# Pooled values of the first six pairs by matmul instead of by a second load, in an attention and mixture kernel on one Trainium2 core

## The chip, the cores and the metric

The kernel runs on one core of one Trainium2 chip. The metric is the device time of one execution in microseconds, the median of a few runs. Engines are named as in the profile: PE is TensorE (PEld its weight loads), DVE is VectorE, ACT is ScalarE, POOL is GpSimd, SP is SyncE, which issues the DMA transfers here.

## The reference, cut to what matters

Eight batches of eight heads with 576 positions of 64 numbers. Attention is the sum of a pooled one (means over 4 positions, repeated 4 times) and a banded one. Its output, with heads side by side, is the input x of a token-shifted feed-forward layer.

```python
q_d = q.reshape(B, H, Sd, 4, D).mean(axis=3)      # the same for k_d, v_d; Sd = 144
out_d = sm_attn(q_d, k_d, v_d)                    # softmax(q k / 8) v
out_up = np.repeat(out_d, 4, axis=2)
mask = np.abs(pos[:, None] - pos[None, :]) < 4
out_local = softmax(where(mask, q k / 8, -1e9)) @ v
x = (out_up + out_local)                          # B, S, H * D = 8, 576, 512
xk = mu_k * x + (1 - mu_k) * x_prev               # x_prev: x one position earlier
xr = mu_r * x + (1 - mu_r) * x_prev
k = np.maximum(xk @ w_k, 0.0)                     # 512 x 1024
v = k * k @ w_v                                   # 1024 x 512
out = sigmoid(xr @ w_r) * v                       # w_r: 512 x 512
```

The three weight matrices arrive as 64-bit floats; the rest is float32.

## The kernel before, in words

**Attention** runs over 32 pairs of heads (four pairs to a batch). `load_raw` fetches q and k of a pair in eight transfers, VectorE transposes them (`turn_q`, `turn_k`), GpSimd adds groups of four columns (`pool_q`, `pool_k`). TensorE computes the banded scores in 24 blocks (`score_pe`) and the pooled scores (`down_last`, `down_pe`) into one PSUM tile; the first four pairs add the mask by a matmul on the identity (L539). Softmax uses VectorE for maxima and sums, ScalarE for exponentials, GpSimd for normalising. `down_turn` transposes the pooled weights on TensorE, `down_copy` evicts them. The values are loaded twice: `load_windows` fetches the overlapping windows of the banded part (`vw`, 128 partitions: window i of 32 positions, 12 tiles of 64), and `load_v4` fetches four successive positions into one partition (`v4`), which GpSimd adds to pooled values (`pool_v`, L517 and L518, into `vd`). `av_pe` multiplies the pooled weights with `vd` (L671, L675) and the banded ones with `vw` (L681), in two row halves with a PSUM tile each. ScalarE evicts the pooled part (`av_up`), VectorE adds the other half's (`av_two`, L707), and `av_out` (L715) writes both into x.

**The feed-forward layer** runs over 18 chunks of 256 positions. Every weight and every x is split into a high and a low part, and three products are summed. A weight block (20 of them, in pairs of 32-bit words) is decoded by `weight_scale` (ScalarE, L377), then three VectorE instructions (L381, L385, L390), then `weight_high` (ScalarE), and the low part is made either by two matmuls on TensorE (`weight_diff`, L401 and L402, the first eight) or by GpSimd (`weight_low`). Mixing of chunk 0 runs on TensorE (`mix_pe`, L761: one call for each of xk and xr and each of four column groups), with ScalarE and VectorE splitting the result (L767, L771); later chunks mix on VectorE and ScalarE. `k_pe` (L800 for chunks 0 and 1, L804 and L806 after), `r_pe` (L850) and `v_pe` (L866) are the three products.

**What sets the order.** Each step is entered as a task with an engine, an assumed duration, what it reads and writes, and a rank. `Plan.order` simulates the five queues, and the rank, plus an entry of the table SHIFT, decides among tasks that could start. The instructions are then held in that order on each engine, DMA issues too. Where the plan sees TensorE idle in the first 100 us, `Plan.fill` puts filler matmuls on the identity (`keep_warm`, L408), as long as one of six PSUM banks is free.

Of the kernel before, what the change touches and what calls it, by code (L numbers as in the profile page):

```python
# [31 lines left out]
VDVE = 0  # L32
SPLIT = 8
# [17 lines left out]
    "r_pe.2": 136.8, "r_pe.3": 138.8, "s.av_out": -2.5, "s.av_two": -20.6, "s.av_up": -3.5, "s.diff": -5,  # L51
    "s.down_copy": 12.5, "s.down_top": -18.3, "s.down_turn": -11.7, "s.k_low": -27, "s.k_relu": -5,
    "s.k_sum": -22.9, "s.mix_add.xr": -105, "s.mix_high.xk": -11.4, "s.mix_low.xk": -44.3, "s.mix_part.xk": 5.4,
    "s.mix_part.xr": -6.5, "s.run_pe": -41.4, "s.score_top": -3.7, "s.score_turn": 16.2, "s.turn_k": 5.3,
# [1134 lines left out]
```

## Time and profile before

| | |
|---|---|
| median of 3 runs | 683.16 us (682.91 to 685.35) |
| the profiled execution | 687.01 us, span 685.2 us, mean granted clock 0.998 |
| busy | PE 660.1, DVE 509.5, ACT 480.8, POOL 295.4 us |
| moved by DMA | 62.19 MB, mean 91 GB/s |
| first k matmul of chunk 0 | 64.18 us |

"Busy" is the time in which an engine ran an instruction. A group row gives line, engine, operation, tiles (output<-input), shape and count, then total busy time and mean ns of one, then idle time before them and who ended it. A timeline row gives start, length, engine, line, tiles, count, and in brackets the idle time before. TensorE rows of plain float32 matmuls count two records for one instruction.

### The profile page before, as it was taken

To read this page: it belongs to the slowest core of one execution; us is meant where nothing else is said; L and a number is where in the kernel's file an instruction comes from. 1 tells how busy PE (TensorE), PEld (TensorE's weight loads), DVE (VectorE), ACT (ScalarE), POOL (GpSimd) and SP (SyncE) were. 2 spreads that over 40 slices of the span, in tenths; PEclk is the share of its full clock that TensorE was granted. 3 is DMA by queue.
4 is the path that set the end of the run, shared out by engine and by line. 5 is a ranking of instruction groups with operands and counts; after the bars stand their busy time and mean duration, and the time that the engine had idled before them with its cause. 6 is when DMAs were issued, how large, how long until landed. Compare 5 with 4: busy or idle time off the path is not lost.

```text
span 685.2 us, 18270 instructions
## 1 busy us (share of the span) xinstructions
PE 660.1 (96%) x7070; PEld 550.8 (80%) x7070; DVE 509.5 (74%) x1020; ACT 480.8 (70%) x1239; POOL 295.4 (43%) x375
## 2 busy tenths in 40 slices
PE   6888989999999999999999999999999999999997
PEld 4566778878788888888888888888888888888886
DVE  3879987889787997988657896599768984666222
ACT  4757877676877877886766767696859686755553
POOL 5545788754274355541515355452645331000000
PEclk9999999999999999999999999999999999999999
DMA  7998998754173435341415234532351100000000
GB/s 150 181 171 247 237 167 151 172 103 107 41 142 71 96 76 116 74 101 18 107 43 123 55 76 85 130 80 66 78 128 37 37 3 32 2 31 32 1 31 32
DMA packets 221593, 62.19 MB, mean 91 GB/s; under 512 B 204730, under 2 KB 214466, under 8 KB 221506
## 3 DMA queue, kind: packets, MB, share of 16 engines
q1 hardware_dynamic: 221506, 61.02, 42.0%
q8 instruction: 56, 0.92, 0.6%
q14 instruction: 31, 0.25, 0.1%
HBM read 51.55 MB, written 9.44 MB: 89 GB/s over the span
## 4 chain that ended last, share of the span: by engine, by line
PE 81%; DVE 9%; DMA 3%; ACT 3%; issue 2%; POOL 1%; SPq 1%; DVEq 0%; POOLq 0%; ACTq 0%
PE acc L866 27%; PE ps_g L804 16%; PE ps_r L850 14%; PE ps_g L806 8%; PE ps_v L681 3%; PE ps_a L544 3%; PE ps_v L671 2%; DMA kraw<-in_k_dram 2%; PE ps_a L611 1%; PE ps_g L800 1%; PE ps_a L604 1%; PE ps_a L549 1%; DMA wk<-in_moe_w_k_dram 1%; ACT L628 1%; PE ps_t L651 1%
## 5 line engine op out<-in xcount | busy, mean ns | idle before, releaser
L866 PE MATMUL acc<-wv,kh 128*128 128x512 f32 x578 | 183.0, 397 | 0.8 <-ACT wv L412 0.8
L804 PE MATMUL ps_g<-xk,wk 128*128 128x512 f32 x512 | 140.8, 397 | 2.5 <-DVE kk L817 1.4
L866 PEld LDWEIGHTS acc<-wv,kh 128*128 128x128 f32 x578 | 103.2, 188 | 20.9 <-ACT wv L412 1.2
L866 PE MATMUL acc<-wv,kl 128*128 128x512 f32 x289 | 113.2, 392 | 0.2 <-DVE kl L839 0.2
L804 PEld LDWEIGHTS ps_g<-xk,wk 128*128 128x128 f32 x512 | 91.1, 188 | 19.9 <-DVE kk L817 2.1
L850 PE MATMUL ps_r<-wr,xr 128*128 128x512 f32 x432 | 103.5, 392 | 0.0
L850 PEld LDWEIGHTS ps_r<-wr,xr 128*128 128x128 f32 x432 | 79.6, 188 | 16.4 <-DVE kk L817 0.2
L839 DVE TENSOR_TENSOR kl<-kk,kh 128x256 fp32r<-128x256 f32 x119 | 65.0, 553 | 37.4 <-ACT kh L832 36.8
L812 ACT ACTIVATE kk<-ps_g 128x256 f32<-128x256 f32 x128 | 46.6, 378 | 59.6 <-PE ps_g L806 54.7
L806 PEld LDWEIGHTS ps_g<-xk,wk 128*128 128x128 f32 x512 | 78.1, 188 | 11.0
L817 DVE TENSOR_TENSOR kk<-ps_g,kk 128x256 f32<-128x256 f32 x128 | 51.4, 414 | 42.7 <-ACT kk L812 41.7
L806 PE MATMUL ps_g<-xk,wk 128*128 128x256 f32 x512 | 80.9, 280 | 0.0
L826 ACT ACTIVATE kk<-kk 128x256 f32<-128x256 f32 x128 | 52.5, 411 | 23.3 <-DVE kk L817 22.7
L839 POOL TENSOR_TENSOR kl<-kk,kh 128x256 fp32r<-128x256 f32 x25 | 20.5, 821 | 108.6 <-ACT kh L832 108.6
L866 PEld LDWEIGHTS acc<-wv,kl 128*128 128x128 f32 x289 | 54.3, 188 | 12.8 <-DVE kl L839 0.6
L832 ACT ACTIVATE kh<-kk 128x256 fp32r<-128x256 f32 x144 | 60.2, 418 | 5.9 <-PE acc L866 1.4
L831 ACT ACTIVATE kk<-kk 128x256 f32<-128x256 f32 x144 | 60.1, 417 | 4.2
L572 POOL TENSOR_TENSOR sm<-sm,mx 128x384 f32<-128x384 f32 x28 | 25.1, 896 | 68.7 <-DVE mx L567 42.0
L508 POOL TENSOR_TENSOR tk<-kz 64x288 f32<-64x288 f32 (+1 forms) x56 | 40.2, 719 | 21.4 <-DVE kz L481 12.2
L587 POOL TENSOR_TENSOR sm<-sm,ssum 128x384 f32<-128x384 f32 x32 | 29.3, 917 | 38.2 <-DVE ssum L583 20.4
L639 POOL TENSOR_TENSOR ad<-ad,sd 128x432 f32<-128x432 f32 x32 | 31.5, 985 | 32.3 <-DVE sd L635 29.4
L517 POOL TENSOR_TENSOR v<-v 128x512 f32<-128x512 f32 x32 | 41.7, 1302 | 6.0 <-DMA v<-in_v_dram 6.0
(125 smaller groups left out, 1274.1 us busy)
## 6 DMA issues: line engine op xcount, KB each, us to landing
vw<-in_v_dram SPq DMA_DIRECT2D x126, 96.0 KB, 3.5
qraw<-in_q_dram SPq DMA_DIRECT2D x128, 72.0 KB, 2.7
kraw<-in_k_dram SPq DMA_DIRECT2D x128, 72.0 KB, 2.7
out_dram<-sig SPq DMA_DIRECT2D x35, 256.0 KB, 2.1
...
```

Of the source, the lines that this page charges most:

```text
L508: nc.gpsimd.tensor_tensor(out=tk[h], in0=k4[:, :, 0:2], in1=k4[:, :, 2:4], op=ALU.add)
L517: eng.tensor_tensor(out=v4[:, :, 0:128], in0=v4[:, :, 0:128], in1=v4[:, :, 128:256], op=ALU.add)
L804: nc.tensor.matmul(ps, w_k_part(p, f, 0), x[:, :, p, :], start=(p == 0), stop=False)
L806: nc.tensor.matmul(ps[:, 0], w_k_part(p, f, 1), x[:, 0, p, :], start=False, stop=(p == NP - 1))
L812: nc.scalar.activation(kk, ps[:, 1], AF.Copy)
L817: nc.vector.tensor_tensor(out=kk, in0=ps[:, 0], in1=kk, op=ALU.add)
L826: nc.scalar.activation(kq[c, f], kq[c, f], AF.Relu)
L831: nc.scalar.activation(kk, kk, AF.Square)
L832: nc.scalar.activation(kh, kk, AF.Copy)
L839: eng.tensor_tensor(out=kl, in0=kk, in1=kh.bitcast(F32), op=ALU.subtract)
L850: nc.tensor.matmul(ps, x[:, y, p, P * t:P * t + P], ws[f"r{p}"][:, w, :], start=(m == 0), stop=(m == len(mm) - 1))
L866: nc.tensor.matmul(accs[c][t][:, h], x[:, P * t:P * t + P], ws[f"v{f}"][:, w, h], start=(f == 0 and m == 0), stop=(f == NF - 1 and m == 2) ...
```

## The change

The pooled values of pairs 0 to 5 (`VPE = 6`) come from the windows already loaded. A window tile `vw` holds 96 positions of each group i of 24 (plus overlap), so a matmul with a 0/1 matrix `pm` sums four neighbouring rows at once. `pool_pe` does that in six matmuls a pair: block b (48 pooled positions) and half j, 128 moving columns, 64 output rows. `pool_copy` evicts the result with two ScalarE copies. The keys then stand in blocks of 48 at partitions 0, 64 (and 0 of a second tile), so `down_turn` turns the weights in blocks of 64 columns, by plain matmuls on half the array's columns instead of transposes, `down_copy` copies 128 partitions, and `av_pe` multiplies the first two blocks in one go; `av_two` falls away for these pairs. `load_v4` and `pool_v` are not issued for them. The mask is loaded into a tile that is free at the start (`bd`), and the mask matmul reads its doubled copy. The table SHIFT is new throughout, so the order on all queues is new; three assumed durations are changed (`score_both` 2.3 to 2.5, `av_pe` 2.0 to 1.5, `down_turn` 0.65 to 0.85).

```diff
+VPE = 6
...
-    "down_copy.4": 33.3, "down_sum.1": -15.2, "down_top.0": 11.1, "down_top.3": 14.9, "fetch_weight.12": 1.7,
+    "down_exp.6": 53.1, "down_sum.1": -35.5, "down_sum.2": -33.1, "down_top.7": 15.4, "down_turn.0": -32.4,
...
-    mask = cp.tile([P, NG, 32], F32, name="mask")
+    mask = bd[:, 6:10, :].rearrange("p u c -> p (u c)").rearrange("p (g c) -> p g c", g=NG)
+    pm = cp.tile([P, 104], F32, name="pm")
...
+    def make_pm():
+        rows = idn.rearrange("p (i r) -> p i r", r=32)[:, :, 3:27].rearrange("p i (t j) -> p i t j", j=4)
+        nc.vector.tensor_reduce(out=pm[:, 40:64].rearrange("p (i t) -> p i t", t=6), in_=rows, axis=AX.X, op=ALU.add)
...
+    def pool_pe(n):
+        d = st[n]
+        d["vp"] = ps = pp.tile([P, 256], F32, tag=plan.bank[f"vp{n}"], name="ps_d", bufs=1)
+        vw = d["vw"].rearrange("p (e g) d -> p e g d", e=2)
+        for b, j in ((0, 0), (1, 0), (0, 1), (1, 1), (2, 0), (2, 1)):
+            i, o = b % 2, 128 * (b // 2)
+            at = 24 * j + (16 if b == 2 else 0)
+            nc.tensor.matmul(ps[64 * i:64 * i + 64, o:o + 128], pm[:, 40 - at:104 - at], vw[:, :, 2 * b + j, :],
+                             start=(j == 0), stop=(j == 1))
+
+    def pool_copy(n):
+        d = st[n]
+        d["vd"] = vd = wp.tile([P, 4, D], F32, tag="vd", name="vd")
+        ps = d["vp"].rearrange("p (x d) -> p x d", d=D)
+        nc.scalar.activation(vd[:, 0:2], ps[:, 0:2], AF.Copy)
+        nc.scalar.activation(vd[0:64, 2:4], ps[0:64, 2:4], AF.Copy)
...
     def down_turn(n):
         d = st[n]
+        if n < VPE:
...
+            for t in (0, 2, 1):
+                for b, k in enumerate((0, 48, 80)):
+                    ps = d["ps_t"][b // 2][64 * (b % 2):64 * (b % 2) + 64]
+                    ak = d["ad"][:, t, k:k + 64]
+                    if t == 1:
+                        nc.tensor.matmul(ps.rearrange("p (e c) -> p e c", e=2)[:, :, 128:144], ak,
+                                         idn[:, 0:32].rearrange("p (e c) -> p e c", e=2), start=True, stop=True)
+                    else:
+                        nc.tensor.matmul(ps[:, 72 * t:72 * t + 128], ak, idn, start=True, stop=True)
+            return
...
-        for r, h in enumerate((slice(0, 64), slice(64, KA))):
+        for r, h in enumerate((slice(0, P),) if n < VPE else (slice(0, 64), slice(64, KA))):
...
-        add("SP", 0.5, R1 - 18, load_v4, n, w=[f"v4.{n % 2}"], dma=1.5)
+        if n >= VPE:
+            add("SP", 0.5, R1 - 18, load_v4, n, w=[f"v4.{n % 2}"], dma=1.5)
...
-            add(*(("DVE", 1.0) if n < VDVE else ("POOL", 2.0)), R1 - 8, pool_v, n, w=[f"v4.{n % 2}"], new=[(f"vd{n}", "vd")])
+            if n < VPE:
+                add("PE", 0.75, R1 - 8, pool_pe, n, r=[f"vw{n}", "pm"], new=[(f"vp{n}", "bank")])
+                add("ACT", 0.6, R1 - 8, pool_copy, n, r=[f"vp{n}"], new=[(f"vd{n}", "vd")])
...
```

Three places where the order moves follow, as lists of instructions in queue order (line, operation, output<-input, shape; `x4` is four in a row). In them `ps_w` and `w` are a weight being decoded, `wk`, `wv`, `wr` the weight blocks, `ps_x` fillers, `ps_t` the turn, `ps_d` the pooled values, `ps_v` attention output, `ps_m` the mix of chunk 0, `ps_a` scores.

TensorE, from the turn of pair 0 to pair 0's `av_pe`, before:

```order
L651 MATMUL ps_t<-idn,ad 112x128
L652 MATMUL ps_t<-idn,ad 112x128
L653 MATMUL ps_t<-idn,ad 112x2x16
L651 MATMUL ps_t<-idn,ad 72x128
L652 MATMUL ps_t<-idn,ad 72x128
L653 MATMUL ps_t<-idn,ad 72x2x16
L408 MATMUL ps_x<-nidn 128x512
L401 MATMUL ps_w<-w_407,idn 128x512
L402 MATMUL ps_w<-wk_427,nidn 128x512
L408 MATMUL ps_x<-nidn 128x512
L671 MATMUL ps_v<-adT,vd 64x144 x4
L675 MATMUL ps_v<-adT,vd 64x144 x2
```

The same place in the changed kernel:

```order
L666 MATMUL ps_t<-idn,ad 64x128 x6
L663 MATMUL ps_t<-idn,ad 64x2x16 x3
L389 MATMUL ps_w<-w_366,idn 128x512
L390 MATMUL ps_w<-wv_379,nidn 128x512
L522 MATMUL ps_d<-vw,pm 64x128 x12
L396 MATMUL ps_x<-nidn 128x512 x2
L666 MATMUL ps_t<-idn,ad 64x128 x6
L663 MATMUL ps_t<-idn,ad 64x2x16 x3
L696 MATMUL ps_v<-adT,vd 64x144 x2
L700 MATMUL ps_v<-adT,vd 64x144 x2
L706 MATMUL ps_v<-bd,vw 64x48 x24
```

The pooling of pairs 0 and 1 and the turn of pair 1 now stand ahead of pair 0's `av_pe`, and the last fillers of the program are the two behind the pooling.

TensorE, ahead of the first k matmul of chunk 0, before:

```order
L761 MATMUL ps_m<-xt,diag 128x256 x4
L671 MATMUL ps_v<-adT,vd 64x144 x4
L675 MATMUL ps_v<-adT,vd 64x144 x2
L681 MATMUL ps_v<-bd,vw 64x48 x24
L401 MATMUL ps_w<-w_997,idn 128x512
L402 MATMUL ps_w<-wk_1007,nidn 128x512
L761 MATMUL ps_m<-xt,diag 128x256 x4
L800 MATMUL ps_g<-xk,wk_131 128x256 x3
```

The same place in the changed kernel:

```order
L706 MATMUL ps_v<-bd,vw 64x48 x24
L389 MATMUL ps_w<-w_1002,idn 128x512
L390 MATMUL ps_w<-wv_1035,nidn 128x512
L786 MATMUL ps_m<-xt,diag 128x256 x2
L612 MATMUL ps_a<-kd,qd_67 128x144
L557 MATMUL ps_a<-kz_71,qT_74 32x32 x48
L619 MATMUL ps_a<-kd,qd_67 64x144 x4
L786 MATMUL ps_m<-xt,diag 128x256 x4
L825 MATMUL ps_g<-xk,wk_601 128x256 x3
```

Pair 4's scores, which stood behind four units of k and one of v before, are now ahead of the first k matmul; so are eight weight remainders instead of five, and one mix of eight is still to come.

SyncE's queue from the first windows to the third pair's q, before:

```order
L453 DMA vw<-in_v_dram 32x12x64 x3
L372 DMA wv_189<-in_moe_w_v_dram 128x1024
L438 DMA v_77<-in_v_dram 112x2x256
L439 DMA v_77<-in_v_dram 32x2x256
L453 DMA vw<-in_v_dram 32x12x64 x4
L438 DMA v_78<-in_v_dram 112x2x256
L439 DMA v_78<-in_v_dram 32x2x256
L429 DMA qraw<-in_q_dram 32x18x32 x4
```

The same place in the changed kernel:

```order
L441 DMA vw<-in_v_dram 32x11x64
L445 DMA vw<-in_v_dram 29x64
L441 DMA vw<-in_v_dram 32x12x64 x7
L360 DMA wv_271<-in_moe_w_v_dram 128x1024
L360 DMA wk_273<-in_moe_w_k_dram 128x1024
L360 DMA wk_279<-in_moe_w_k_dram 128x1024
L417 DMA qraw<-in_q_dram 32x18x32 x4
```

The windows of two pairs now follow each other, and three weight blocks stand where the second loads of values stood. VectorE's queue moved with them: ahead of the last `xk` subtraction (L771, now L796) it holds 12 shifts and 24 combinations of weights instead of 9 and 17, 11 transposes of q and k instead of 8, 5 pooled row maxima instead of 4, two of xr's four subtractions instead of three, and no `av_two` instead of 4.

More of the change, by code (lines that the diff above doesn't have):

```diff
@@ L42 @@
 SHIFT = {
[8 rows of a table removed]
[L51 to L54, printed above, removed]
[29 rows of a table removed]
[6 rows of a table added]
+    "s.down_sum": -1.8, "s.k_high": -2.6, "s.mix_part.xr": 0.9, "s.store_mul": -1.5, "sav_out.25": 14,
[11 rows of a table added]
 }
@@ L133, in add @@
     def add(self, eng, us, rank, f, *args, r=(), w=(), new=(), dma=0.0, lock=None):
-        t = dict(eng=eng, us=us, rank=rank + self.shift(f.__name__, args), f=f, args=args, new=list(new), dma=dma, deps=set(),
+        t = dict(eng=eng, us=us, rank=int((rank + self.shift(f.__name__, args)) * 1000 + 1000000.5) / 1000 - 1000, f=f, args=args, new=list(new), dma=dma, deps=set(),
                  id=len(self.tasks), name=f.__name__, lock=lock)
@@ L305, in attention_moe @@
     mask2 = cp.tile([P, NG, 2, 32], F32, name="mask2")
-    qTs = [cp.tile([P, 592], F32, name=f"qT{i}") for i in range(2)]
+    qTs = [cp.tile([P, 584], F32, name=f"qT{i}") for i in range(2)]
     v4s = [cp.tile([P, 4, 256], F32, name=f"v4{i}") for i in range(2)]
+    pm = cp.tile([P, 104], F32, name="pm")
     def load_consts():
@@ L336, in turn_sign, with clear_pm @@
         nc.scalar.activation(nidn, idn, AF.Copy, scale=-1.0)
+    def clear_pm():
+        nc.gpsimd.memset(pm, 0.0)
+    def make_pm():
+        rows = idn.rearrange("p (i r) -> p i r", r=32)[:, :, 3:27].rearrange("p i (t j) -> p i t j", j=4)
+        nc.vector.tensor_reduce(out=pm[:, 40:64].rearrange("p (i t) -> p i t", t=6), in_=rows, axis=AX.X, op=ALU.add)
     def double_mask():
@@ L538, in score_pe @@
             for e in range(2):
-                nc.tensor.matmul(ps[:, S1 * e:S1 * e + 32 * NG], idn, mask, start=True, stop=False)
+                nc.tensor.matmul(ps[:, S1 * e:S1 * e + 32 * NG].rearrange("p (g c) -> p g c", g=NG), idn,
+                                 mask2[:, :, e, :], start=True, stop=False)
         for j in range(4 * NG):
@@ L643, in down_turn @@
         d = st[n]
+        if n < VPE:
+            if n < NP:
+                d["ps_t"] = [pp.tile([P if kt == 0 else 64, 288], F32, tag=plan.bank[f"pst{n}{kt}"], name="ps_t", bufs=1) for kt in range(2)]
+            else:
+                ps = pp.tile([P, 1024], F32, tag="att", name="ps_t", bufs=1)
+                d["ps_t"] = [ps[0:m, 512 * kt:512 * kt + 288] for kt, m in enumerate((P, 64))]
+            for t in (0, 2, 1):
[5 more added lines that the diff above has]
+                                         idn[:, 0:32].rearrange("p (e c) -> p e c", e=2), start=True, stop=True)
+                    else:
+                        nc.tensor.matmul(ps[:, 72 * t:72 * t + 128], ak, idn, start=True, stop=True)
+            return
         if n < NP:
@@ L658, in down_copy @@
         d["adT"] = aT = wp.tile([P, 2, 288], F32, tag="adT", name="adT", bufs=1)
-        nc.scalar.activation(aT[0:KA, 0, :], d["ps_t"][0], AF.Copy)
+        m = P if n < VPE else KA
+        nc.scalar.activation(aT[0:m, 0, :], d["ps_t"][0], AF.Copy)
         nc.scalar.activation(aT[0:64, 1, :], d["ps_t"][1][0:64], AF.Copy)
@@ L918, in pair_scores @@
             add("POOL", 1.12 if n < SPLIT else 2.06, R - 6, pool_k, n, r=[f"kT{i}"], new=[(f"kd{n}", "kd")])
-            add(*(("DVE", 1.0) if n < VDVE else ("POOL", 2.0)), R1 - 8, pool_v, n, w=[f"v4.{n % 2}"], new=[(f"vd{n}", "vd")])
+            if n < VPE:
+                add("PE", 0.75, R1 - 8, pool_pe, n, r=[f"vw{n}", "pm"], new=[(f"vp{n}", "bank")])
+                add("ACT", 0.6, R1 - 8, pool_copy, n, r=[f"vp{n}"], new=[(f"vd{n}", "vd")])
+            else:
+                add(*(("DVE", 1.0) if n < VDVE else ("POOL", 2.0)), R1 - 8, pool_v, n, w=[f"v4.{n % 2}"], new=[(f"vd{n}", "vd")])
         if part == 1:
@@ L932, in pair_scores @@
             add("ACT", 0.95, R1 - 4, spread, n, r=[f"at{n}"], w=["bd"])
-            add("PE", 0.65, R1 - 7, down_turn, n, r=[f"ad{n}"],
+            add("PE", 0.85 if n < VPE else 0.65, R1 - 7, down_turn, n, r=[f"ad{n}"],
                 new=[(f"pst{n}{kt}", "bank") for kt in range(2)] if n < NP else [(f"pst{n}0", "att")])
@@ L941, in pair_scores @@
                 add("POOL", 0.1, R1, new_x, b, new=[(f"xt{b}", "xt")], w=[(f"xt{b}", i) for i in range(NP)])
-            add("DVE", 0.27, R1 + 2, av_two, n, r=[f"pv{n}b"], w=[f"up{n}"])
+            if n >= VPE:
+                add("DVE", 0.27, R1 + 2, av_two, n, r=[f"pv{n}b"], w=[f"up{n}"])
             add("DVE", 0.82, R1 + 2, av_out, n, r=[f"pv{n}", f"pv{n}b", f"up{n}"], w=[(f"xt{b}", p)])
@@ L1069, in begin_all @@
     def begin_all():
-        add("SP", 1.0, -10000.0, load_consts, w=["mask", "idn"])
+        add("SP", 1.0, -10000.0, load_consts, w=["mask", "idn", "bd"])
         add("POOL", 4.2, -110, clear, w=["kT0", "kT1", "qT0", "qT1", "qd.0", "qd.1", "bd"])
@@ L1080, in attention_moe @@
     add("ACT", 0.3, -60, turn_sign, r=["idn"], w=["nidn"])
-    add("POOL", 1.0, -60, double_mask, r=["mask"], w=["mask2"])
+    add("POOL", 0.1, -109, clear_pm, w=["pm"])
+    add("DVE", 0.2, -108, make_pm, r=["idn"], w=["pm"])
+    add("POOL", 1.0, -60, double_mask, r=["mask", "bd"], w=["mask2"])
     for i in range(len(WORDER)):
@@ L1086, in attention_moe @@
         pair_scores(n, 0)
-        add("PE", 2.3, at_run[n], score_both, n, r=[f"qd.{n % 2}", f"kd{n}", f"qT{n % 2}", f"kT{n % 2}"],
+        add("PE", 2.5, at_run[n], score_both, n, r=[f"qd.{n % 2}", f"kd{n}", f"qT{n % 2}", f"kT{n % 2}", "mask2"],
             new=[(f"ps{n}", "att")])
         pair_scores(n, 1)
-        add("PE", 2.0, after(n), av_pe, n, **av_of(n))
+        add("PE", 1.5, after(n), av_pe, n, **av_of(n))
         pair_scores(n, 2)
```

52 rows, old and new, of the table SHIFT are left out of this document.

## The prediction

> **What bounds the kernel now.** I read the page first (busy shares and the chain that ended last), then busy time by 10 us windows, then TensorE's timeline at the start, then what TensorE waits for.
>
> ```profile
> span 685.2 us, 18270 instructions
> PE 660.1 (96%) x7070; PEld 550.8 (80%) x7070; DVE 509.5 (74%) x1020; ACT 480.8 (70%) x1239; POOL 295.4 (43%) x375
> ...
> PE 81%; DVE 9%; DMA 3%; ACT 3%; issue 2%; POOL 1%; SPq 1%; DVEq 0%; POOLq 0%; ACTq 0%
> ...
> 0.00:10.00 10.00, 6.09 (x17) 4.10 (x17) 2.43 (x4) 3.26 (x5) 6.79 (x21) 1.00 0.78 163
> 10.00:20.00 10.00, 8.39 (x132) 5.70 (x132) 6.35 (x11) 7.45 (x25) 3.66 (x7) 1.00 0.91 157
> 20.00:30.00 10.00, 7.52 (x188) 5.54 (x188) 8.10 (x20) 7.69 (x25) 5.34 (x7) 1.00 1.11 186
> 30.00:40.00 10.00, 8.59 (x208) 6.51 (x198) 7.60 (x16) 4.24 (x13) 6.07 (x9) 1.00 0.79 139
> 40.00:50.00 10.00, 7.46 (x134) 5.92 (x133) 7.34 (x18) 4.91 (x14) 4.38 (x6) 0.88 1.23 186
> 50.00:60.00 10.00, 9.02 (x150) 7.00 (x149) 9.57 (x22) 7.52 (x22) 6.68 (x7) 0.95 0.89 261
> 60.00:70.00 10.00, 8.39 (x50) 6.46 (x49) 9.42 (x18) 8.00 (x18) 5.62 (x5) 1.00 0.88 225
> ...
> 64.18 3.11 PE L800 MATMUL ps_g<-xk,wk 128*128 128x256 f32 x24 [0.99 <-DVE xk L771]
> ```
>
> A window's row gives its length, then the busy time of PE, PEld, DVE, ACT and POOL, the granted clock, the DMA share and GB/s. TensorE is the bound (96% busy, 81% of the chain), so any TensorE work added after the start costs its full length. The start is another stage: until 64.18 us, when the first feed-forward matmul of chunk 0 runs, TensorE does pair work and fillers, while DMA stands at 0.8 to 1.2 and VectorE climbs to 9.57 of 10. That first matmul is released by VectorE (`mix_rest`, L771). So the time is: arrival of the first k matmul, plus TensorE work left after it, plus waits after it.
>
> The waits that remain after it, all above 0.3 us, and the largest stretch of fillers (matmuls on the identity, L408):
>
> ```profile
> PE ps_g L804 <- DVE kk L817: 1.4, 3, 0.8
> PE ps_a L549 <- issue: 1.3, 1, 1.3
> PE ps_g L804 <- DVE xk L792: 1.1, 1, 1.1
> PE ps_g L800 <- ACT kk L823: 0.9, 2, 0.6
> PE acc L866 <- ACT wv L412: 0.8, 1, 0.8
> PE ps_a L604 <- POOL kd L509: 0.6, 1, 0.6
> PE ps_g L800 <- ACT wv L412: 0.4, 1, 0.4
> ...
> 73.01 2.43 PE L408 MATMUL ps_x<-nidn 128*128 128x512 f32 x10
> ```
>
> That is 6.5 us of waits and 2.43 us of fillers, 8.9 us in all.
>
> **Pooled values on TensorE.** Per pair, `pool_pe` adds 6 float32 matmuls with 128 moving columns, each on half of the array's columns; `down_turn` becomes 6 such matmuls and 3 short ones. No row has that shape. The nearest is the banded score, which uses quarters of the columns; the mask matmul, on the whole array, is the bound without any overlap.
>
> ```profile
> L544 PE MATMUL ps_a<-kz,qT 128*32 128x64 f32 x1152 | 21.1, 221 | 0.0
> ...
> L539 PE MATMUL ps_a<-mask,idn 128*128 128x192 f32 x16 | 3.3, 326 | 0.0
> ...
> 85.65 0.27 PE L651 MATMUL ps_t<-idn,ad 128*112 128x128 f32 x1
> ...
> 86.31 0.71 PE L866 MATMUL acc<-wv,kh 128*128 128x512 f32 x2
> ```
>
> A float32 matmul leaves two records. L544: 21.1/1152 x 2 = 0.037 us for 64 columns on a quarter, so 128 columns on a half take 4 x 0.037 = 0.147 us. L539: 3.3/8 x 128/192 = 0.275 us without overlap. I take 0.147, since L544 also runs all 128 rows. Pooling is then 6 x 0.147 = 0.88 us a pair (bound 1.65). The turn is 0.88 + 3 x 0.037 = 0.99 (bound 1.86), against 86.31 - 85.65 = 0.66 now: +0.33 (bound +1.20). In `av_pe` six matmuls become four, two of them over twice the rows; I take 0 (no more than 0.2 either way). So +1.2 us a pair (bound +2.85), 7.2 us for six (bound 17.1).
>
> Here a page speaks against the change. "TensorEngine Tiling" in the Trainium skill (Restrictions) says that column tiling disables the transpose mode for float32, and "TensorE: Matmul & The Clock Gate" (Terms) calls that mode 4 times faster for float32. The trace has one record for a transpose and two for a plain matmul. By the page's factor, as an estimate, the four transposes' part of the 0.66 us, some 0.5, would become 2.0 us, the turn would lie at its upper bound, and the sum at rival 4's.
>
> What it takes away: the second load of values, its two GpSimd additions and one VectorE addition.
>
> ```profile
> L517 POOL TENSOR_TENSOR v<-v 128x512 f32<-128x512 f32 x32 | 41.7, 1302 | 6.0 <-DMA v<-in_v_dram 6.0
> ...
> L518 POOL TENSOR_TENSOR vd<-v 128x256 f32<-128x256 f32 x32 | 26.5, 830 | 38.5 <-PE ps_v L675 36.9
> ...
> L707 DVE TENSOR_TENSOR up<-ps_v,up 128x144 f32<-128x144 f32 x32 | 9.4, 294 | 3.0 <-ACT up L703 3.0
> ...
> L703 ACT ACTIVATE up<-ps_v 128x144 f32<-128x144 f32 x32 | 9.1, 284 | 7.1 <-PE ps_v L681 7.0
> ```
>
> GpSimd loses 6 x 2.13 = 12.8 us, VectorE 6 x 0.29 = 1.8 us, the DMA queue 6 x 288 KB = 1.73 MB (about 10 us at the 139 to 186 GB/s of the first 50 us) and 12 issues. ScalarE gains 12 evictions the size of L703, 3.4 us; its cover is that it is 33 to 77% busy until 60 us, and without that cover they would cost their 3.4 us. None of the saved time is on TensorE. The small mask and `pm` edits cost a matmul nothing; `make_pm` is one reduction on VectorE (taken as 0.2 us) while it waits for its first data.
>
> **When the first k matmul comes.** Before, VectorE is busy 41.39 us in the six windows to 60 us and 4.2 x 0.942 = 3.95 us more to 64.2: 45.3 us, 18.9 idle. The order puts more in front of the last `xk` subtraction: 7 more weight combinations, 3 more shifts, 3 more transposes of q and k, one more row maximum (reduction and scaling), `make_pm`, and 4 `av_two` and one `xr` subtraction fewer.
>
> ```profile
> L381 DVE TENSOR_SCALAR ps_w<-ps_w 128x512 int32<-128x512 int32 x20 | 13.7, 690 | 9.0 <-ACT ps_w L377 9.0
> ...
> L467 DVE STREAM_TRANSPOSE qT<-qraw 128x576 f32<-128x576 f32 x32 | 24.5, 765 | 2.1 <-DMA qraw<-in_q_dram 1.6 <-DMA v<-in_v_dram 0.4 <-issue 0.2
> ...
> L618 DVE TENSOR_REDUCE mxd<-ps_a 128x3 f32<-128x432 f32 x32 | 19.3, 603 | 29.1 <-PE ps_a L544 25.9 <-PE ps_a L549 2.6 <-PE ps_a L611 0.5
> ...
> L619 DVE TENSOR_SCALAR mxd<-mxd 128x3 f32<-128x3 f32 x32 | 9.1, 283 | 1.1
> ...
> L771 DVE TENSOR_TENSOR xr<-ps_m,xr 128x256 fp32r<-128x256 f32 x4 | 1.7, 418 | 0.5 <-ACT xr L767 0.5
> ```
>
> 10 x 0.690 (a combination runs over the same 512 elements as a shift, and I price it so) + 3 x 0.765 + 0.603 + 0.283 + 0.2 - 4 x 0.294 - 0.418 = 8.7 us, so 54.0 us of VectorE work stands ahead. In the first 30 us VectorE was idle 30 - 16.88 = 13.1 us; queries and keys now load ahead of the weights, but the second pair's k, and then the third pair's q behind three weights, still have to land, so I keep 13.1; GpSimd's clearing of the value tiles, moved ahead of that of qT, falls into these idle microseconds (7.6 of them are in the first window). The other 37.1 us can run at 95% (50 to 70 us before) or at before's mean of 30 to 64.2 us, 28.4/34.2 = 83%: 39.1 or 44.7 us. Between its waits VectorE now has more weights to decode, so I take the middle, 90%: 41.2 us. The first k matmul comes at 71.2 us, 7.0 later; the ends are 69.1 (+4.9) and 74.7 (+10.5).
>
> A wait is added: the pooling of pair 1 waits for pair 1's windows, and pair 1's turn and pair 0's `av_pe` are queued behind it on TensorE; the adds to x and the first mix wait for those.
>
> ```profile
> 28.85 0.47 PE L671 MATMUL ps_v<-adT,vd 64*64 64x144 f32 x8 [1.39 <-POOL vd L518]
> ```
>
> Before, 4.0 MB stood in the queue up to the second load behind that `av_pe`; now 3.1 MB up to pair 1's windows. In proportion they land near 21 to 22 us, and two poolings, two evictions and the spread (3 to 4 us) end at about 26: the wait is covered, and what is late next is the third pair's q.
>
> **What is left then.** Ahead of that moment TensorE has done more. The rows that price it:
>
> ```profile
> 69.10 1.02 PE L401 MATMUL ps_w<-w,idn 128*128 128x512 f32 x2
> ...
> 70.19 1.58 PE L800 MATMUL ps_g<-xk,wk 128*128 128x256 f32 x12
> ...
> 76.00 0.51 PE L604 MATMUL ps_a<-kd,qd 128*128 128x144 f32 x2 [0.57 <-POOL kd L509]
> ...
> 77.81 1.13 PE L401 MATMUL ps_w<-w,idn 128*128 128x512 f32 x2
> ...
> 61.19 2.00 PE L761 MATMUL ps_m<-xt,diag 128*128 128x256 f32 x8 [0.32 <-DVE xt L715]
> ```
>
> Three more weight remainders at 70.19 - 69.10 = 1.09 (3.3 us), pair 4's scores at 77.81 - 76.00 = 1.81, four pairs' pooling and turns (4 x 1.2 = 4.8), and one mix of eight still to do (-1.0): 8.9 us. Added in all: 7.2. Left is 7.2 - 8.9 = 1.7 us less than before. Without overlap it is 17.1 - (8.9 + 6.6) = 1.6 us more.
>
> Of the 8.9 us of later waits and fillers, those go whose cause is now done early: the fillers and L509 of pair 4 (3.0; its scores already stand ahead), the two on decoded `wv` (1.2; VectorE is 8.7 us of work ahead), chunk 2's `xk` (1.1), and half of the instruction wait (0.6). That is 5.9 us. The ends are 8.9 and 3.0 (the first term alone).
>
> **Sum:** +7.0 - 1.7 - 5.9 = -0.6 us. The profiled execution took 687.01 us, 1.8 around its span; the median of the runs, 683.16, is 3.85 below it. Applied to the median: 682.6 us. The most favourable ends give +4.9 - 1.7 - 8.9 = -5.7 (677.5), the least +10.5 + 1.6 - 3.0 = +9.1 (692.3). About 0.5% (3.4 us) is what a measurement of this kernel can tell from no change.
>
> **Rivals.**
> 1. *The prepared work pays fully (faster).* VectorE runs at 95%, and every later wait goes except half of the instruction one: +4.9 - 1.7 - 8.3 = -5.1, 678.1 us. For it: weights stand between all waits in the new order. Against it: 73 to 76% in 30 to 50 us, with weights in the queue there as well.
> 2. *VectorE's in-order queue waits more (slower).* A weight's combination ahead of pair work holds that back until the weight has landed. At 80% the 37.1 us last 46.4: 76.4, 12.2 late, and +12.2 - 1.7 - 5.9 = +4.6, 687.8 us. It decides (+3.4) at 82%. For it: the row of 40 to 50 us, with DMA at 1.23. Against it: 1.73 MB less to load.
> 3. *Fillers run out and the clock falls (slower).* Ahead of the first k matmul stood 55 fillers; now 40, none after the two behind the pooling of pairs 0 and 1. The one long bare gap before was followed by half clock:
>
> ```profile
> 45.87 0.48 PE L604 MATMUL ps_a<-kd,qd 128*128 128x144 f32 x2 [2.54 <-issue]
> ...
> 48.00:50.00 2.00, 2.00 (x19) 1.58 (x17) 1.17 (x3) 1.02 (x2) 1.54 (x2) 0.50 1.31 142
> ```
>
> Each such episode would hold up scores or a turn by 1 to 1.5 us (a turn is 0.66 us at full clock); three or four on the way give -0.6 + 4.5 = +3.9, 687.1 us. Against it: the window of 30 to 40 us, with shorter gaps, kept 1.00. "TensorE: Matmul & The Clock Gate" in the Trainium skill (Part 1) says that the clock halves after an idle window of about 3.4 us; here 2.54 us without work sufficed.
> 4. *No overlap between the column halves.* 1.6 + 1.7 = 3.3 us on the work left: -0.6 + 3.3 = +2.7, 685.9 us, within 0.5%. For it: no row of this shape; against it: L544's four quarters.
>
> **Chances.** My forecast 0.44, rival 1 0.28, rival 2 0.13, rival 3 0.08, rival 4 0.07. Faster by over 0.5%: 0.28; within: 0.44 and most of rival 4, 0.50; slower: 0.22. Cutting a tenth at either side, inside the favourable end and rivals 2 and 3, leaves 678.0 to 688.5 us; the forecast's own range is 680 to 686.
>
> **What would show it.** The first k matmul (now L825) at 70 to 73 us, released by VectorE `xk`; pool matmuls under `ps_d` at 0.13 to 0.18 us each; a turn near 1.0 us; named waits and fillers after the first k matmul down to 2 to 4 us; granted clock 0.9 or more in each 10 us window. I am wrong if the first k matmul comes before 68 or after 76 us, if the waits after it don't shrink, or if new waits appear past 250 us.

## The result: about 1% slower, and the profile after

The changed kernel takes 691.57 us (median of 4 runs, 690.83 to 694.44), the kernel before 684.25 us; the ratio is 1.0115, with a 95% interval from 1.0077 to 1.0153. A second comparison, on another chip session with more runs of before, gave 1.0083 [1.0052, 1.0114]. By these ratios it is about 6 to 8 us slower, where I had forecast 682.6 us and a range to 688.5.

The head of the page, and then busy time by 10 us windows, of the changed kernel (columns as before: PE, PEld, DVE, ACT, POOL, granted clock, DMA share, GB/s):

```profile
span 689.0 us, 18347 instructions
PE 666.4 (97%) x7153; PEld 555.9 (81%) x7153; DVE 513.3 (74%) x1015; ACT 481.9 (70%) x1251; POOL 283.7 (41%) x364
...
30.00:40.00 10.00, 7.11 (x122) 4.65 (x123) 8.48 (x15) 5.43 (x14) 3.27 (x6) 0.88 0.94 180
40.00:50.00 10.00, 10.00 (x207) 6.65 (x205) 8.36 (x19) 7.29 (x21) 2.83 (x4) 0.95 1.14 249
50.00:60.00 10.00, 7.69 (x101) 6.09 (x97) 9.64 (x22) 7.46 (x24) 4.01 (x5) 0.90 1.00 206
60.00:70.00 10.00, 9.28 (x178) 6.57 (x177) 7.84 (x14) 5.40 (x12) 4.65 (x5) 0.76 1.14 241
```

TensorE's busy time went up by 6.3 us, although 25 fillers fewer ran (40 instead of 65). The granted clock is below 1 in four windows, where before it was in two, and 0.76 in the last of them.

Then TensorE's timeline. The rows are those of the pooling of pairs 0 and 1, of two bare stretches and what follows them, of the first k matmul, and of one turn at full clock:

```profile
23.07 1.96 PE L522 MATMUL ps_d<-vw,pm 128*64 128x128 f32 x24
...
36.48 0.51 PE L612 MATMUL ps_a<-kd,qd 128*128 128x144 f32 x2 [2.17 <-POOL kd L497]
...
57.87 1.61 PE L666 MATMUL ps_t<-idn,ad 128*64 128x128 f32 x11 [2.31 <-DVE xt L740]
59.07 0.42 PE L663 MATMUL ps_t<-idn,ad 128*64 128x32 f32 x2
59.27 0.42 PE L666 MATMUL ps_t<-idn,ad 128*64 128x128 f32 x1
59.49 0.58 PE L663 MATMUL ps_t<-idn,ad 128*64 128x32 f32 x4
60.66 0.75 PE L696 MATMUL ps_v<-adT,vd 128*64 128x144 f32 x4 [0.59 <-ACT adT L685]
...
71.95 1.67 PE L825 MATMUL ps_g<-xk,wk 128*128 128x256 f32 x12 [2.08 <-DVE xk L796]
...
76.58 0.98 PE L666 MATMUL ps_t<-idn,ad 128*64 128x128 f32 x11
77.29 0.30 PE L663 MATMUL ps_t<-idn,ad 128*64 128x32 f32 x2
77.39 0.27 PE L666 MATMUL ps_t<-idn,ad 128*64 128x128 f32 x1
77.50 0.37 PE L663 MATMUL ps_t<-idn,ad 128*64 128x32 f32 x4
77.80 3.08 PE L825 MATMUL ps_g<-xk,wk 128*128 128x256 f32 x24
```

The first k matmul comes at 71.95 us and is released by VectorE's `xk`, as forecast. A turn takes 77.80 - 76.58 = 1.22 us; the same turn at half clock (57.87 to 59.49 + 0.58) takes over 2 us. Ahead of each of the two half-clock stretches TensorE stood bare, without work, for 2.2 to 2.3 us.

Busy time on both sides of the first k matmul, of the kernel before and of the changed one:

```profile
64.18:685.20 621.02, 610.15 (x6254) 514.43 (x6254) 464.02 (x926) 442.57 (x1133) 260.74 (x320) 1.00 0.37 80
```

```profile
71.95:689.00 617.05, 607.45 (x6169) 513.05 (x6169) 460.80 (x910) 437.03 (x1121) 252.17 (x310) 1.00 0.33 75
```

Behind it, the changed kernel is only 4.0 us shorter, for a start 7.8 us later. That is the +3.8 us between the two profiles. The median moved further, since the profile of before that I worked from was one of its longer executions: a second one, 682.5 us long, has its first k matmul at 62.38 us.

### The profile page after: what moved, and what is told of

It reads as the page before. It is cut to its first block, busy times and chain, and to the rows that moved or that the text cites. A ratio compares the mean times of both kernels' runs of the same rounds, so it can differ in the third digit from the quotient of the medians.

```text
span 689.0 us, 18347 instructions
## 1 busy us (share of the span) xinstructions
PE 666.4 (97%) x7153; PEld 555.9 (81%) x7153; DVE 513.3 (74%) x1015; ACT 481.9 (70%) x1251; POOL 283.7 (41%) x364
## 4 chain that ended last, share of the span: by engine, by line
PE 79%; DVE 5%; ACT 2%; issue 1%; POOL 0%; DVEq 0%; ACTq 0%; POOLq 0%
PE acc L891 27%; PE ps_g L829 16%; PE ps_r L875 14%; PE ps_g L831 8%; PE ps_v L706 3%; PE ps_a L552 3%; PE ps_g L825 2%; PE ps_v L696 2%; PE ps_a L619 1%; PE ps_a L612 1%; PE ps_t L675 1%; PE ps_t L677 1%; PE ps_t L676 1%; PE ps_v L700 1%; ACT L636 1%
## 5 line engine op out<-in xcount | busy, mean ns | idle before, releaser
L829 PE MATMUL ps_g<-xk,wk 128*128 128x512 f32 x512 | 141.7, 398 | 1.5 <-DVE xk L817 1.1
L829 PEld LDWEIGHTS ps_g<-xk,wk 128*128 128x128 f32 x512 | 92.3, 188 | 20.5 <-issue 1.7
L864 DVE TENSOR_TENSOR kl<-kk,kh 128x256 fp32r<-128x256 f32 x119 | 66.9, 563 | 33.8 <-ACT kh L857 33.3
L864 POOL TENSOR_TENSOR kl<-kk,kh 128x256 fp32r<-128x256 f32 x25 | 19.5, 780 | 115.9 <-ACT kh L857 86.2
L580 POOL TENSOR_TENSOR sm<-sm,mx 128x384 f32<-128x384 f32 x28 | 23.5, 838 | 68.6 <-DVE sd L642 41.9
L647 POOL TENSOR_TENSOR ad<-ad,sd 128x432 f32<-128x432 f32 x32 | 34.1, 1065 | 28.6 <-DVE sd L643 23.5
L626 DVE TENSOR_REDUCE mxd<-ps_a 128x3 f32<-128x432 f32 x32 | 19.3, 603 | 29.8 <-PE ps_a L552 29.1
```

The costliest lines, as they stand in the source:

```text
L647: nc.gpsimd.tensor_tensor(out=ad, in0=ad, in1=sd[:, :, None].broadcast_to([P, 3, 144]), op=ALU.mult)
L829: nc.tensor.matmul(ps, w_k_part(p, f, 0), x[:, :, p, :], start=(p == 0), stop=False)
L864: eng.tensor_tensor(out=kl, in0=kk, in1=kh.bitcast(F32), op=ALU.subtract)
```

## The experiments

Two theories stood against each other at the start. One: the new order puts VectorE's and TensorE's work ahead of the first k matmul and gets too little back. Two: TensorE is bare more often without the lost fillers, falls to half clock, and so loses time. That the pooling is expensive wherever it stands was the third. Ratios below are to the kernel before in the same session, with 95% intervals.

**The same kernels again.**

> The kernel before once more, unchanged, for a second profile of it: the first one took 687.01 us, 2.8 above the median of its runs. If the extra lay in the start (loads that landed late there), an execution near 684 us shows its first k matmul 2 to 3 us before the 64.18 us of the first profile, and the work after it as long as there (621.0 us to the end of the span). Rival: the extra lies behind the first k matmul, which then stands at 64 us again.

> The changed kernel once more, unchanged, so that the next kernels can be compared with it on the same chip. Ratio to before 1.010 to 1.012, first k matmul at 71 to 73 us, half clock again somewhere in 36 to 42 and in 58 to 65 us.

Before: 685.73 us, 1.0002 [0.9976, 1.0028]; its first k matmul at 62.38 us, 620.1 us to the end. Of the 2.7 us by which the first profile is longer, 1.8 lie in the start, as expected, and 0.9 behind it. After: 691.67 us, 1.0083; first k matmul at 72.76 us, half clock again at 38.7 to 42.1 and 59.1 to 66.0, and once more at 72.8 to 76.2. Over the 104 runs of the kernel before in the five sessions of these comparisons, those at clock 1.000 took 684.8 us (30 runs), those at 0.995 687.6 (19 runs): a fit gives 0.75 us of time for a microsecond of clock lost (span times 1 minus clock). That is a correlation and not a price: a load that lands late would leave TensorE bare, and so lengthen the start and lower the clock at once. The changed kernel's ten runs had clocks of 0.987 to 0.995.

**Fillers back in the changed kernel.** The first kernel puts fillers ahead of the two bare stretches, the second at four places.

```diff
+        if at in (("score_both", 2), ("down_turn", 3)):
+            kept.append(dict(eng="PE", f=warm_att, args=(9,)))
+        if at == ("av_pe", 3):                                   # second kernel only
+            kept.append(dict(eng="PE", f=warm_att, args=(2,)))
+        if at == ("k_pe", 0, 0):                                 # second kernel only
+            kept.append(dict(eng="PE", f=warm_att, args=(8, "b4")))
```

> The changed kernel with nine fillers each ahead of pair 2's scores and pair 3's turn, where TensorE stood bare for 2.2 and 2.3 us and half clock followed; they write the score tile, which is free there. Theory that the lost fillers matter: granted clock 1.00 through both stretches, about 3.3 us less TensorE time in 57 to 66 us (turn, pair 3's values and a weight remainder took twice their time), VectorE waits less for it, first k matmul 2 to 3 us earlier, total 2 to 3 us below the changed kernel. Rival, that VectorE's and the DMA's work sets the start: first k matmul within 1 us of the changed kernel's, total within 1 us.

> As after_warm, with two fillers more ahead of pair 3's values and eight ahead of the first k matmul, where TensorE stood bare for 2.0 us in every profile of the changed kernel. Theory that half clock is the larger part of the loss: no half clock up to 84 us, first k matmul at 70 to 72 us, total 1 to 3 us below the changed kernel (ratio 1.004 to 1.007). Rival, that what the fillers hold up is lost again or that the order itself is slow: ratio 1.008 or more.

The first: 691.16 us, 1.0065 [1.0039, 1.0090]. Its start was at full clock and the first k matmul at 70.77 us, 1.2 to 2.0 us earlier, less than the 2 to 3 expected, and the median stood within 1 us of the changed kernel's, as the rival said; but its profile has half clock at 86.2 to 89.6 and 123.7 to 127.1 us, behind instruction waits in a run of small matmuls (1.47 and 1.56 us). It is inconclusive by itself. The second: **688.39 us, 1.0043 [1.0026, 1.0060]**, clock 0.996 to 1.000 in its 12 runs, first k matmul at 70.90 us: close to its theory. Windows of 8 us, first of the changed kernel's second profile, then of this one:

```profile
36.00:44.00 8.00, 7.03 (x132) 4.22 (x134) 6.52 (x11) 3.89 (x13) 3.02 (x6) 0.79 1.00 207
...
60.00:68.00 8.00, 7.41 (x161) 5.45 (x162) 5.88 (x11) 4.44 (x10) 2.36 (x3) 0.63 1.07 245
68.00:76.00 8.00, 5.61 (x56) 4.33 (x44) 7.76 (x15) 3.92 (x13) 7.02 (x7) 0.80 0.85 157
```

```profile
36.00:44.00 8.00, 7.15 (x176) 4.60 (x174) 7.25 (x15) 5.01 (x16) 3.30 (x6) 1.00 1.07 228
...
60.00:68.00 8.00, 7.78 (x181) 5.37 (x180) 7.72 (x14) 5.03 (x11) 3.67 (x5) 1.00 1.09 266
68.00:76.00 8.00, 7.22 (x48) 5.87 (x47) 7.69 (x16) 5.90 (x19) 6.56 (x8) 1.00 0.95 221
```

So 28 useless matmuls more make the changed kernel about 3.2 us faster. Against before it loses 0.43% instead of 0.83 to 1.15%: half clock was half of its loss or a little more, and the rest stays at full clock. A clock of 0.79 over 8 us is 8 x 0.21 / 0.5 = 3.4 us at half clock, and 0.63 is 5.9 us.

**Fillers away, without and with pooling.** In the kernel before, and in its order with pairs 0 to 3 pooled on TensorE (see below), groups of fillers are left out of the order.

```diff
+    fillers = [t for t in emitted if t["f"] is keep_warm]
+    emitted = [t for t in emitted if t not in fillers[5:]]      # third kernel: fillers[5:8]
```

> The kernel before without its last four groups of fillers (8, 4, 6 and 10 of the 65; the changed kernel has 40, this has 37). Theory that fillers hold the clock: half clock for 3.4 to 6.8 us in one or two more places between 40 and 80 us, 2 to 4 us more (ratio 1.003 to 1.006). Rival: the bare time costs nothing, and the 2.43 us of fillers behind the first k matmul are partly saved: ratio 0.997 to 1.001.

> The order of before with pairs 0 to 3 pooled on TensorE, without the last four groups of fillers (28 of 65). In the kernel before their removal left the time where it was (0.998), and pooling four pairs too (0.999); TensorE loses 2.4 us of fillers behind the first k matmul: 683 to 686 us, ratio 0.995 to 0.999. Rival: with the pooling the start has less room, and half clock there costs 1 to 3 us: ratio 1.000 to 1.004.

> As old_order_pe4_bare, with the ten fillers behind the first k matmul kept: only the 18 between pair 1's values and pair 3's turn are left out. Theory that half clock in the start costs once TensorE also pools there: first k matmul at 66 to 68 us, half clock in 44 to 60 us, ratio 1.003 to 1.007. Rival, that the start absorbs it and the ten fillers behind were what counted: first k matmul at 64 to 65 us, ratio 0.998 to 1.001.

A second group of four fillers, ahead of pair 0's scores, fell out with its equal later on, so the traces of the three kernels count 33, 33 and 43 fillers of 65. Without pooling: 684.95 us, 0.9981 [0.9956, 1.0007], although the clock fell to 0.985 to 0.996; the theory that it would cost 2 to 4 us falls. With pooling: 691.87 us, 1.0075 [1.0045, 1.0104], above both of my figures. With pooling and the ten late fillers kept: 689.93 us, 1.0055 [1.0039, 1.0071], first k matmul at 67.77 us, as the theory said. The same with all 65 fillers is 0.999 (next). Pair 3's turn with its pooling, and the work up to the mix behind it, first with all fillers and then with 43:

```profile
54.09 0.98 PE L683 MATMUL ps_t<-idn,ad 128*64 128x128 f32 x11 [0.36 <-POOL ad L664]
...
55.22 1.07 PE L541 MATMUL ps_t<-vw,v 128*64 128x128 f32 x11
56.21 2.00 PE L804 MATMUL ps_m<-xt,diag 128*128 128x256 f32 x8
...
64.52 1.69 PE L843 MATMUL ps_g<-xk,wk 128*128 128x256 f32 x12 [1.00 <-DVE xk L814]
```

```profile
55.96 1.22 PE L683 MATMUL ps_t<-idn,ad 128*64 128x128 f32 x11 [2.72 <-POOL ad L664]
...
57.58 1.95 PE L541 MATMUL ps_t<-vw,v 128*64 128x128 f32 x11
59.45 2.23 PE L804 MATMUL ps_m<-xt,diag 128*128 128x256 f32 x8
...
67.77 1.45 PE L843 MATMUL ps_g<-xk,wk 128*128 128x256 f32 x10 [1.00 <-DVE xk L814]
```

Turn and pooling take 2.1 us with fillers and 3.5 without, and the first k matmul comes 3.2 us later. Without pooling it didn't move:

```profile
63.53 4.55 PE L800 MATMUL ps_g<-xk,wk 128*128 128x256 f32 x36 [0.99 <-DVE xk L771]
```

That is between the 62.38 and 64.18 us that it had with all fillers. So the start that has no pooling absorbed half clock, and the start that has it did not. One thing differs besides the pooling: the first kernel had half clock at 15.5 to 18.9, 29.1 to 32.5 and 53.0 to 56.4 us, the third at 15.6 to 19.0, 46.3 to 49.7 and 56.6 to 60.0, so part of the difference may lie in where it fell.

**The pooling in the order of before.** No second load, no additions for it; the pooling stands right behind the turn, in the same PSUM banks. The pooling code is that of the changed kernel; the first three lines below are against it, the others against the kernel before.

```diff
-                d["ps_t"] = [pp.tile([P if kt == 0 else 64, 288], ...
+                d["ps_t"] = [pp.tile([P if kt == 0 else 64, 416], ...
...
+            pool_pe(n)                       # at the end of down_turn, into columns 288:416
...
+        if name in ("load_v4", "pool_v", "av_two") and n < VPE:
+            pass
+        elif name == "down_copy" and n < VPE:
+            kept += [t, dict(eng="ACT", f=pool_copy, args=(n,))]
```

> The order of the kernel before, with the mechanism of the change: for pairs 0 to 5 no second load, no GpSimd addition and no VectorE addition; the pooling matmuls stand right behind the pair's turn, in the same two PSUM banks, and ScalarE evicts them behind the turned weights. Theory that the order makes the change slow: first k matmul no later than before (60 to 64 us), and the two pairs behind it cost 1.6 us each, so ratio 0.998 to 1.005. Rival, that the pooling makes it slow wherever it stands: first k matmul at 66 us or later, ratio 1.007 or more.

> As old_order_pe6 with pairs 0 to 3 alone, so that no TensorE work is added behind the first k matmul. Theory that pooling ahead of the first k matmul is covered and frees the DMA: 0 to 3 us below the kernel before (ratio 0.996 to 1.000), and 3 us below old_order_pe6. Rival, that the pooling sits on the path in the start: above old_order_pe6 less 3 us, 2 to 6 us above the kernel before.

> As old_order_pe6, where the 0/1 matrix stood in a buffer that was loaded over before pair 5 was pooled; here it stands in the mask's tile. The same time as old_order_pe6, ratio 0.998 to 1.003, first k matmul at 62 to 65 us. If the order is not what makes the change slow, 1.007 or more.

> As old_order_pe6b, where the mask's values were left in the outer columns of the 0/1 matrix, with those columns cleared: one small clearing on GpSimd more. 686 to 687 us, ratio 0.998 to 1.003.

Six pairs: 686.46, 686.30 and 685.57 us, ratios 0.9999 [0.9980, 1.0018], 0.9994 [0.9970, 1.0017] and 0.9990 [0.9974, 1.0006]; four pairs: 685.41 us, 0.9990 [0.9970, 1.0009]. (In the first, pair 5's pooled values come from a spoiled matrix, in the second the matrix holds mask values at its edges; the matmuls are the same in all three.) First k matmul at 64.2 to 64.6 us, clock 0.998 to 1.000 in all 48 runs. The third theory falls: with what it takes away, the pooling costs nothing measurable in the order of before. None of these beats the kernel before, and four pairs are 1 us below six, not the 3 us expected.

**The order of the changed kernel without the pooling.**

```diff
-        if n < VPE:
+        if n < 0:                        # in down_turn; likewise in down_copy and av_pe
...
+        if name == "pool_pe":
+            kept.append(dict(eng="POOL", f=pool_v, args=(n,)))
+        elif name == "av_out" and n < VPE:
+            kept += [dict(eng="DVE", f=av_two, args=(n,)), t]
+        elif name == "load_windows" and n < VPE:
+            kept += [t, dict(t, f=load_v4, dma=1.5)]
```

> The order of the changed kernel, instruction for instruction, with its mechanism undone: the six pairs' values are loaded a second time (behind their windows) and added by GpSimd in the place where TensorE pooled them, the turn is by transposes again, and VectorE adds the second row half's part again. Theory that the order makes it slow (more VectorE work ahead of the first k matmul): first k matmul at 71 to 75 us, and since TensorE saves 1.6 us for each of the two pairs behind it, total 2 to 6 us above the kernel before (ratio 1.003 to 1.009). Rival, that the pooling on TensorE makes it slow: first k matmul at 62 to 66 us, ratio 1.000 within 0.003.

> As new_order_v4, but each second load is issued only when the addition that used its buffer before is in the queue (there, later pairs' loads stood ahead of earlier pairs' additions, which then waited for them). The order of the changed kernel without its mechanism: TensorE loses 1.7 us of work a pair (pooling 1.02, turn 0.56, values 0.14), 10.3 us in all. Theory that the order delays the first k matmul whatever computes the values: it comes at 70 to 74 us, and only the two pairs behind it give time back, 3.4 us: total 2 to 5 us above the kernel before (ratio 1.003 to 1.008). Rival, that TensorE's added work is what costs: the first k matmul comes 4 us or more earlier than in the changed kernel and the total is that of the kernel before or less (ratio 1.000 or under).

> The changed kernel in its own order, with pairs 4 and 5, the two that are pooled behind the first k matmul, loaded a second time and turned by transposes as before. By the price in the trace TensorE has 2 times 1.7 = 3.4 us less to do there: total 3 to 4 us below the changed kernel (ratio to before 1.003 to 1.006). Rival, that this work lies in waits which stay: less than 1 us below it (ratio 1.008 to 1.010).

723.03 us (1.0533 [1.0492, 1.0573]; pairs 0 to 5 add the values of later pairs), 700.38 us (1.0191 [1.0152, 1.0230]) and 695.62 us (1.0115 [1.0072, 1.0158]). All three are slower than the changed kernel or no faster; neither theory said so. In the last two the inserted additions hold GpSimd's queue up: pair 5's turn waits 7.6 and 6.95 us for GpSimd behind the first k matmul, so their totals say nothing on the price. In the second, without the pooling, the new order's first k matmul is at 75.15 us, no earlier than with it. But that start isn't the new order alone either: the inserted additions stand ahead of pair 1's normalising there, pair 1's turn waits 3.69 us for it, and half clock lasts from 55.4 to 69.0 us. So these runs don't show whether the order alone makes the start late.

**Less VectorE work ahead, in the new order.** The first kernel moves two weights' decoding behind the last `xk` subtraction, the others (the edit below) all that the first k matmul doesn't need, from two points on.

```diff
+    stay = lambda t: t["eng"] == "SP" or t.get("id") in needed     # needed: ancestors of the first k_pe
+    emitted = (emitted[:a] + [t for t in emitted[a:b] if stay(t)] + [t for t in emitted[b:] if unit(t)]
+               + [t for t in emitted[a:b] if not stay(t)] + [t for t in emitted[b:] if not unit(t)])
```

> The changed kernel with the decoding of two weight blocks (v4 and v5, six VectorE instructions, 4.1 us) moved from ahead of the last subtraction of xk to right behind it. Theory that VectorE's queue sets the first k matmul: it comes 3 to 4 us earlier than in the changed kernel (68 to 69 us); if nothing else is late then, the total falls by as much. Rival, that the moment is set by loads and by TensorE at half clock: less than 1.5 us earlier. Rival on the payback: it comes earlier, but the total falls by less than 1 us, since VectorE is 95% busy until 100 us and the decoded weights are late there instead.

> The changed kernel with the last part of the start in another order: from the values of pair 2 on, all that the first k matmul doesn't need (a weight remainder, pair 4's scores and three of its steps on VectorE, ten instructions of weights there, most of xr's mix) is moved behind it, and the first three units of k stand together. About 11 us of VectorE's work and 4.9 us of TensorE's go from ahead of it to behind it. Theory that the work put ahead sets the first k matmul and is not paid back: it comes 5 to 8 us earlier than in the changed kernel (64 to 67 us), and the total falls by 2 to 4 us (ratio to before 1.004 to 1.007). Rival, that pairs 0 to 3 and half clock set it: less than 3 us earlier. Rival, that the work ahead is paid back in full: it comes 5 to 8 us earlier, and the waits behind it grow by as much (ratio 1.009 to 1.013).

> As xk_first, reaching back to pair 2's turn: two more weights (six more instructions on VectorE and one more remainder on TensorE) and the rest of xr's mix go behind the first k matmul. Theory that work ahead sets it: another 1 to 4 us earlier (61 to 65 us). The total stays at that of xk_first within 2 us, if VectorE has room behind; it is 3 us or more above it, if these weights are then late for v.

First k matmul at 71.34, 69.05 and 68.65 us; totals 697.18 us (1.0150 [1.0113, 1.0186]), 707.08 us (1.0302 [1.0278, 1.0326]) and 711.82 us (1.0375 [1.0348, 1.0402]). My first theory falls on both counts, and so do those of the second and third kernel. Taking 4 us off VectorE's queue brought 0.6 to 1.4 us, 11 us brought 2.9 to 3.7. Two windows of the second kernel, ahead of its first k matmul:

```profile
56.00:64.00 8.00, 4.99 (x76) 4.16 (x77) 1.65 (x4) 1.43 (x5) 0.00 (x0) 0.65 0.94 163
64.00:72.00 8.00, 6.12 (x19) 4.15 (x17) 3.06 (x6) 0.77 (x2) 0.00 (x0) 0.50 0.99 235
```

VectorE is busy 1.65 and 3.06 of 8 us there, so it isn't the limit; TensorE, emptied of weights and scores, runs at half clock from 58.4 to 72.0 us. So these kernels don't tell how early the moment would be at full clock. And the work ahead is repaid: without it TensorE waits for a weight (5.2 us) behind the first k matmul. In the first kernel one wait is of my own making: ScalarE's share of the two weights stands ahead of the first `k_relu`, and TensorE waits 6.21 us for it.

**Twice the pooling.**

```diff
-        for b, j in ((0, 0), (1, 0), (0, 1), (1, 1), (2, 0), (2, 1)):
+        for b, j in 2 * ((0, 0), (1, 0), (0, 1), (1, 1), (2, 0), (2, 1)):
```

> The changed kernel with every pooling matmul issued twice: 72 matmuls instead of 36, 6.1 us of TensorE work more at the 1.02 us a pair seen in the trace. Theory that TensorE work ahead of the first k matmul is covered by VectorE's work: only pairs 4 and 5, which are pooled behind it, count, +2.0 us. Rival, that pooling sits on the path in the start too (the turn and the values wait for it): +4 to +6 us and a first k matmul 2 to 4 us later.

693.56 us, 1.0126 [1.0096, 1.0156] against 1.0083 in the same session: +1.9 us by the medians, as the first theory said (+2.9 by the ratios); first k matmul at 73.90, 1.1 to 2.0 us later, where that theory had it covered. The intervals overlap, so this is a pointer only.

## Why the prediction was wrong, point by point

The step that failed is the setting aside of rival 3: the sum has no term for the clock. Two accounts show how much of the miss it was. The first is of TensorE over the whole span. Work is the time in which the trace has a matmul other than a filler running. "Lost to half clock" is half of the part of it that ran while the granted clock was 0.5. The fillers' rows are here those of the kernel before, of the changed kernel, and of the fillers added to it in its last version:

```profile
L408 PE MATMUL ps_x<-nidn 128*128 128x512 f32 x65 | 19.0, 436 | 3.5 <-ACT nidn L336 3.5
```

```profile
L396 PE MATMUL ps_x<-nidn 128*128 128x512 f32 x40 | 11.7, 447 | 3.5 <-ACT nidn L316 3.5
```

```profile
L396 PE MATMUL ps_x<-nidn 128*128 128x512 f32 x40 | 12.2, 461 | 3.4 <-ACT nidn L316 3.4
...
L1149 PE MATMUL ps_x<-nidn 128*128 128x512 f32 x28 | 7.5, 406 | 0.0
```

| profiles | span | work | lost in it to half clock | work at full clock | idle and fillers |
|---|---|---|---|---|---|
| before, mean of 685.2 and 682.5 | 683.85 | 642.5 | 1.5 | 641.0 | 41.4 |
| changed, mean of 689.0 and 691.6 | 690.3 | 655.9 | 5.6 | 650.3 | 34.4 |
| changed, fillers at four places | 686.6 | 651.3 | 0 | 651.3 | 35.3 |
| order of before, six pairs pooled (last version) | 684.2 | 648.6 | 0 | 648.6 | 35.6 |

Forecast: 7.2 us more work, and since the sum was -0.6, 7.8 us less idle time and fillers. Measured: 7.0 less idle time and fillers, 9.3 more work at full clock, and 4.1 more lost to half clock. The three errors, 0.8, 2.1 and 4.1, make up the miss of 7.0 us against the profiles.

The second account is in the terms of the sum, from the same profiles (moment of the first k matmul, work behind it without fillers, idle time and fillers behind it):

| term | forecast | measured, means of two | with fillers at four places |
|---|---|---|---|
| first k matmul later | +7.0 | +9.1 | +7.6 |
| work left behind it | -1.7 | +0.6 | -0.5 |
| waits and fillers behind it | -5.9 | -3.2 | -4.4 |
| sum | -0.6 | +6.5 | +2.7 |

All three terms missed the same way, and with the clock kept up each comes nearer to its forecast. What is left then, about 3.3 us, is 0.6 in the start, 1.2 of work behind it and 1.5 of waits and fillers there.

- **The clock (rival 3, to which I gave 0.08).** The mechanism and the order of its price (+4.5, against 4.1 in the account and 3.2 us that the fillers gave back) were there, but I set it aside because the window of 30 to 40 us "kept 1.00". One profile can't say that: the second profile of before has half clock at 30.6 to 34.0 us and none at 48 to 52. And half clock that is free in one kernel needn't be in the next: with fillers left out, the order of before lost nothing measurable without the pooling and 0.55 to 0.75% with it. "TensorE: Matmul & The Clock Gate" of the Trainium skill (Part 1) puts the change behind an idle window of about 3.4 us; the window runs freely and isn't reset when a kernel starts. The traces agree with the length, 3.4 us at a time or a multiple of it, and the place changed from run to run; but here it came behind bare stretches of only 1.90 to 2.31 us in the two profiles of the changed kernel.
- **The price of the pooling.** Forecast 1.2 us a pair. Two poolings stand from 23.07 to the next start at 24.96, so 0.95 each (1.02 where one stands alone), against 0.88; the turn costs +0.56, not +0.33; pair values about 0.14 more, not 0. By rows that is 1.7 a pair, by the first account 1.55. Column halves do overlap (without overlap a pooling would take 1.65 us), so rival 4 is refuted. And the estimate in the prediction from the Trainium skill's pages, "TensorEngine Tiling" (Restrictions) and "TensorE: Matmul & The Clock Gate" (Terms), put the turn at its upper bound of 1.86 us: it is 1.22.
- **The first k matmul.** As a moment it came near (71.2 forecast, 71.95 and 72.76 measured), as a delay it was 2.1 us short, since the 64.18 us that I counted from belong to one of the longer executions of before. VectorE's work ahead was sized about right, 52.5 us against 54.0. But the moment isn't shown to follow from it: 4 to 11 us less in that queue moved it by 0.6 to 3.7 us, with TensorE at half clock instead. That the moment came near is luck in part.
- **Work left** behind it is more by 2.3 us than forecast; half clock behind the first k matmul in one of the two profiles is part of that (72.8 to 76.2 us, about 1.5 us of work lost there, 0.7 in the mean). **Later waits** fell by 3.2 us, not 5.9. The waits on `wv` and on pair 4's keys went, as forecast; the one on chunk 2's `xk` (L829) and the instruction wait (L557) stayed, and small ones on `ad` and `kl` grew:

```profile
PE ps_a L557 <- issue: 1.3, 2, 1.0
PE ps_g L829 <- DVE xk L817: 1.1, 1, 1.1
PE ps_t L675 <- POOL ad L647: 0.7, 1, 0.7
PE acc L891 <- DVE kl L864: 0.6, 1, 0.6
PE ps_g L825 <- ACT kk L848: 0.5, 1, 0.5
```

- **Rival 2** (VectorE's queue, first k matmul at 76.4) isn't what happened: it came at 71.95 and 72.76. **Rival 1** needed the waits to go, and more than half of them stayed.

What stays open is the other half of the loss. At full clock the changed kernel still takes 0.43% more than before, while the same pooling in the order of before takes no measurable time more. The new order has 1.7 to 2.7 us more work by the first account (650.3 and 651.3 against 648.6); I have no row that shows where. Nor is it shown what makes pairs 0 to 3 later in the new order, apart from half clock: at full clock its first k matmul still came at 70.8 to 70.9 us, against 64.2 to 64.6 in the old order.
